# One mixer block on one core: two weight quarters loaded into the dead place of k, another split of the inverse shuffles, the normed input written later, and a new table of due times

## The chip, the cores and the metric

The kernel runs on one core of a Trainium2 chip. The metric is device time in microseconds (us): the median of three runs, 181.79 us, with 181.39 us the lowest and 182.12 us the highest. A profile was taken of one further execution. The engines are named as in the profile: PE (matrix multiplications; its weight loads are shown apart, as PEld), DVE (vector engine), ACT (scalar engine), POOL (GpSimd) and SP (which only issues DMAs here).

## The reference, cut to what matters

With S = 2048 positions and D = 448 channels, a gated long convolution is followed by a layer norm and an MLP that mixes positions:

```python
def _A_ref(q, k, v, shift_k, ssm_k, ssm_D):
    ...
        k_shift = k_shift + k_pad[:, t:t + S, :] * shift_k[:, ks - 1 - t][None, None, :]
    kv = k_shift * v
    ...
    y_f = kv_f * kf_f[None, :, :, :]
    ...
    y = y + kv * ssm_D[None, None, :]
    return q * y

def _B_ref(x, w1, b1, w2, b2):
    h = _layernorm(x, axis=-1)
    u = jnp.einsum("bsd,sf->bdf", h, w1) + b1
    u = _gelu(u)
    y = jnp.einsum("bdf,fs->bds", u, w2) + b2
    return (lambda x, *d: x.transpose(*d))(y, 0, 2, 1)

x = A_q
h = x + _A_ref(_layernorm(x, axis=-1), A_k, A_v, A_shift_k, A_ssm_k, A_ssm_D)
h2 = h + _B_ref(_layernorm(h, axis=-1), B_w1, B_b1, B_w2, B_b2)
```

W1 is 2048 x 1792 and W2 is 1792 x 2048, both bf16. The products y_f are a convolution of length 4096 along the positions; the kernel does it with small Fourier matrices on PE.

## The kernel before

**Layout.** Position s = 16 q + r lies in partition q (128 of them) and row r (R = 16 rows), so x, k and v are each 16 rows of 448 channels in every partition. All of SBUF is one tile, `arena`, cut by hand into byte ranges that are used again: k lies at bytes 0 to 14335 of each partition (`o_KH`), the transposed filter KT at 17024 to 31359, and the first half of W1 (`W1A`, hidden units 0 to 895, 16 rows of 1792 bytes) at 0 to 28671. So rows 0 to 7 of `W1A` cover exactly k, and rows 8 to 15 cover part of KT.

**Stages, in order.** (1) Inputs are loaded; k is transposed on PE (L936) and shifted, kv is formed (L955, L961). (2) "k1" and "u1": the first Fourier stage of the filter and of kv (L1015), copied out of PSUM (L1025), and moved between partitions by DMAs inside SBUF, the forward shuffles (L1031). (3) "k2" and "u2": the second stage (L1050). (4) "i1": sixteen products on DVE (L1083), eight groups of inverse matmuls (L1095) and sixteen copies out of PSUM (L717 when ACT does it, L720 when DVE does), each group giving two columns j = 2jj and 2jj+1 of `TU`. (5) Each column goes through an inverse shuffle into `TZ`: a big DMA from POOL for partitions 0 to 111 and a small one from SP for partitions 112 to 127 (L1119). The last pair of columns, 14 and 15, is split further by halves h (L1108): for h = 0 POOL issues both big DMAs and SP both small ones; for h = 1 POOL issues the big one of column 14, SP the big one of column 15, and ACT both small ones. The big DMAs fill rows 0 to 13 of `TZ` (group "zpool"), the small ones rows 14 and 15 ("zsp"). (6) "i2": the second inverse stage, two matmuls a row (L1215), reads a row of `TZ`. It can't begin before all big DMAs have landed, since each of them writes 8 partitions of all its rows. (7) Then for each row: times 1/sigma plus one (the gate, L1224 on ACT or L1226 on DVE), times (x - mean) (L1234), a sum and a sum of squares (L1262 on ACT), a chain of five small POOL operations for each pair of rows (L1272, L1275, L1277, L1282, and the power L1286), and the normed row Q (L1293). Rows 0 to 3 take another way: their normed x, `XN`, is prepared before (L1185 on ACT, L1187 on DVE; tag "xn") in the place of `TK`, and one operation (L1244) combines it with the matmul's result. Rows 0 and 1 have groups of their own with mean and variance from DVE (L1250, L1253, L1282), so POOL only has the power to do. (8) "mlp": seven accumulators in PSUM take Q row by row against `W1A` (L1340), then the other seven against `W1B` (L1350), GELU on ACT (L1330), and the second layer against W2 (L1362) with the last additions on DVE (L1365) and the stores.

**Statistics of x** (tag "q"): L1155 and L1157 on DVE, L1160 and L1163 on POOL, rows in pairs.

**Filler.** "warm" issues 34 matmuls whose result nobody uses (L1129), and "i2" two more groups of one; all of them are tied to one another in order.

**What sets the order.** Nothing is issued by hand. `op(...)` records each operation with what it reads and writes, and a planner (`schedule`) makes a list for each engine: whenever an engine is free in the planner's own clock, it takes, among the operations that are ready there, the one with the earliest due time; only among equal ones does the longer chain of work that hangs on it count. The due times are the table `WHEN`, one entry for each step of a tag. For operations that ACT or DVE can do, `WHERE` says a (ACT), d (DVE) or f (either, by the planner's clock). `after=` adds a full dependency, `safter=` one that only orders the planner's list. The lists are fixed in the program: on the chip an engine runs its list in order and waits with everything behind it when the next one isn't ready.

**W1 and W2.** `emit_w1_load` loads each half of W1 in four quarters of four rows (L1313 for `W1A`, L1317 for `W1B`), `emit_w2_load` W2 in four parts (L1324). All twelve are issued by SP and have `after=[shuf["zpool"]]`: none starts before the big inverse shuffles have landed.

Of the kernel before, what the change touches and what calls it, by code (L numbers as in the profile page):

```python
# [12 lines left out]
    "dummy": (69,),  # L13
    "tables": (172, 222, 238, 115, 211, 90, 258, 324,),
    "loads": (189, 214, 205, 290, 237, 82, 264, 277, 251, 276, 104, 283, 244, 317, 322,),
    "kv": (253, 110, 128, 123, 135, 121, 85, 66, 113, 159, 149, 191, 230, 266, 235, 142, 275,),
    "kT": (114, 112, 155, 152, 96, 80, 177, 176,),
    "k1": (188, 194, 229, 249, 190, 192, 213, 216, 218, 221, 227, 241, 185, 255, 269, 284,),
    "k2": (93, 139, 239, 168, 180, 225, 273, 295, 321, 320, 313, 314, 262, 293, 318, 315,),
    "u1": (250, 270, 274, 304, 287, 299, 311, 316, 268, 271, 296, 298, 301, 303, 306, 307,),  # L20
    "xload": (291, 182, 300, 223,),
    "ct": (100,),
    "bias": (178,),
    "q": (248, 233, 76, 233, 234, 329, 330, 332, 333,),
    "u2": (89, 97, 118, 141, 132, 137, 117, 91, 199, 164, 246, 219, 145, 156, 278, 281,),
    "i1": (151, 43, 55, 45, 52, 46, 58, 51, 74, 67, 64, 61, 150, 88, 56, 54,),
    "xn": (215, 265, 285, 232, 207, 256,),
    "w1a": (208, 148, 107, 323,),
    "w1b": (130,),
    "warm": (184, 183, 158, 65, 62, 83, 57, 125, 126, 127, 63, 59, 86, 209, 210, 187, 179, 106, 129, 167, 161, 157,  # L30
        153, 206, 193, 181, 196, 120, 101, 72, 32, 0, 47, 169,),
    "i2": (170, 1, 327, 10, 15, 6, 138, 4, 49, 9, 14, 3, 7, 243, 11, 2, 13, 17, 242, 25, 108, 103, 111, 282, 40, 163,
        220, 197, 12, 31, 257, 247, 286, 35, 60, 99, 312, 160, 140, 254, 308, 44, 41, 68, 22, 20, 98, 133, 245, 261,
        38, 29, 204, 289, 162, 18, 26, 240, 305, 294, 202, 154, 102, 263, 259, 201, 309, 39, 302, 328, 16, 147, 71,
        200, 326, 325, 27, 42, 30, 174, 94, 297, 75, 267, 195, 203, 331, 36, 272, 186, 260, 136, 92, 165, 24, 116,
        292, 217, 53, 231, 95, 70, 124, 105, 23, 48,),
    "w2": (198,),
    "mlp": (280, 166, 171, 212, 50, 28, 134, 122, 119, 226, 37, 112, 81, 21, 19, 5, 87, 144, 34, 84, 33, 131, 79, 8,
        146, 78, 77, 175, 224, 310, 109, 236, 228, 279, 143, 173, 252, 73, 288, 319,),
# [11 lines left out]
    "xn": "afdf",  # L51
    "i2": "fffadaaaaffd",
# [518 lines left out]
def _build(nc, A_q, A_k, A_v, A_shift_k, A_ssm_k, A_ssm_D, B_w1, B_b1, B_w2, B_b2, out):  # L571
# [5 lines left out]
    Bsz, S, D = A_q.shape  # L577
# [22 lines left out]
    o_TK = 31360  # L600
# [25 lines left out]
    with ctx:  # L626
        sch = _Sched(nc, ctx, n_dma_sems=112, small_off=SMALL)
        op = sch.op
# [97 lines left out]
        def emit_tables():  # L726
# [49 lines left out]
            for a, b_, c_ in ((0, 112, 14), (112, 128, 2)):  # L776
                op("pool", lambda e, W, a=a, b_=b_, c_=c_: e.iota(gcm[:, a:b_], [[0, 8], [512, c_]], base=512 * 14 * (a > 0),
# [5 lines left out]
            for k, (b0, st_) in enumerate(((2048, -2048), (2048, 2048), (0, 2048))):  # L783
                for a, b_ in (((0, 128),) if k == 0 else ((0, 112), (112, 128))):
                    op("pool", lambda e, W, k=k, b0=b0, st_=st_, a=a, b_=b_: e.iota(
                        cph[:, 128 * k + a:128 * k + b_], [[st_, 2], [0, (b_ - a) // 2]], base=b0, channel_multiplier=0),
                       w=[(o_gc + 1536 + 512 * k, 512, "cp%d" % k)], n=128, est=190.0)
# [252 lines left out]
        shuf = {}  # L1040
# [30 lines left out]
        i1_last = []  # L1071

        def emit_products_i1():
            for jj in range(R // 2):
# [16 lines left out]
                for h in range(2):  # L1091
# [7 lines left out]
                    evac(lambda jj=jj, h=h: TU[:, 2 * jj:2 * jj + 2, h, :], lambda b=bs[h]: Ppair(b),  # L1099
                         [(o_TU + (4 * jj + h) * DB, DB), (o_TU + (4 * jj + 2 + h) * DB, DB)], bs[h], 2 * D)  # L1100
                if jj == R // 2 - 1:
                    for h in range(2):
# [322 lines left out]
```

## Time and profile before

| what | value |
|---|---|
| median of the runs | 181.79 us |
| the profiled execution, its own time | 182.27 us |
| its span, first to last instruction | 180.2 us |
| share of the span busy: PE, DVE, ACT, POOL | 95%, 58%, 51%, 35% |
| matmuls of the MLP (L1340, L1350, L1362), number | 112, 112, 238 |
| SP issues all loads by | 9.4 us |
| first forward shuffle issued | 26.40 us |
| first inverse shuffle issued | 62.29 us |
| last big inverse shuffle issued by SP | 79.00 us |
| first matmul of i2 | 83.97 us |
| first weight DMA (L1313) issued | 83.94 us |

The span is what the instructions cover; the rest of the time of an execution, 2.07 us here, lies around it. PE's busy share is modelled, and shorter pauses of a matmul stream are hidden in it, so stages are best read from what an engine waited for. A wait is named after whatever came last by the profile.

### The profile page before, as it was taken

What the parts mean: (1) busy time and instruction counts of PE and PEld (TensorE: products, weight loads), DVE (VectorE), ACT (ScalarE), POOL (GpSimd) and SP (SyncE); (2) the same over time, 40 slices, a digit from 0 to 9 for tenths busy, and PEclk for the clock granted to TensorE, in tenths of its full rate; (3) what the DMA queues carried; (4) which work ended last, traced back from release to release, by engine and by line L of the source; (5) the groups of instructions that cost most, each with busy time, mean ns of one, the idle gap of its engine ahead of it and who ended that gap; (6) DMA issues with size and microseconds to landing.
All of it is one profiled execution on the core that took longest, in us unless ns stands there. A gap on an engine that the chain in (4) does not pass through costs nothing.

```text
span 180.2 us, 3395 instructions
## 1 busy us (share of the span) xinstructions
PE 170.7 (95%) x1333; PEld 97.5 (54%) x1333; DVE 104.8 (58%) x182; ACT 91.2 (51%) x129; POOL 63.2 (35%) x157
## 2 busy tenths in 40 slices
PE   6999999999889999898898999999999999999994
PEld 2888746543223332244343545556565677777784
DVE  7998677669889999999998645000000053322331
ACT  3897375689899999953985264710221100000000
POOL 8641209562950148797389953000000000000000
DMA  5997008686784947663999999990000001111122
GB/s 178 389 409 251 5 4 308 225 312 186 262 266 131 365 126 210 201 206 89 375 378 401 405 417 421 417 415 28 4 0 0 0 0 40 66 51 51 51 76 76
DMA packets 15347, 35.11 MB, mean 195 GB/s; under 512 B 3724, under 2 KB 9388, under 8 KB 15332
## 3 DMA queue, kind: packets, MB, share of 16 engines
q1 hardware_dynamic: 12068, 28.00, 41.8%
q0 software_dynamic: 3072, 6.80, 11.9%
q8 instruction: 10, 0.16, 0.4%
q10 hardware_dynamic: 192, 0.11, 0.2%
q14 instruction: 5, 0.04, 0.1%
HBM read 22.05 MB, written 1.84 MB: 133 GB/s over the span
## 4 chain that ended last, share of the span: by engine, by line
PE 65%; DVE 12%; ACT 10%; DMA 5%; POOL 3%; issue 2%; SPq 1%; DVEq 0%; POOLq 0%
PE ps L1362 23%; PE ps L1350 12%; PE ps L1340 9%; PE ps L955 7%; DVE arena L1083 5%; DMA arena<-arena 5%; PE ps L1015 4%; ACT arena L1025 4%; ACT arena L717 2%; PE ps L994 2%; PE ps L1050 2%; ACT arena L718 2%; PE ps L1095 1%; POOL arena L1286 1%; ACT arena L826 1%
## 5 line engine op out<-in xcount | busy, mean ns | idle before, releaser
L1362 PE MATMUL ps<-arena 128*128 128x448 bf16 (+2 forms) x238 | 43.5, 342 | 0.0
L1365 DVE SCALAR_TENSOR_TENSOR arena<-ps,arena 128x448 bf16<-128x448 f32 (+2 forms) x17 | 11.1, 656 | 54.2 <-PE ps L1362 54.2
L1362 PEld LDWEIGHTS ps<-arena 128*128 128x128 bf16 x238 | 32.9, 145 | 10.1 <-ACT arena L1330 0.8
L1340 PE MATMUL ps<-arena 128*128 128x448 bf16 x112 | 23.4, 353 | 0.6 <-DVE arena L1293 0.6
L1031 POOL DMA_DIRECT2D arena<-arena x32 | 17.5, 553 | 17.3 <-ACT arena L1025 16.3
L717 ACT CAST arena<-ps 128x896 bf16<-128x896 f32 x28 | 23.3, 979 | 0.4
L1350 PE MATMUL ps<-arena 128*128 128x448 bf16 x112 | 22.8, 352 | 0.0
L1025 ACT CAST arena<-ps 128x896 bf16<-128x896 f32 x22 | 18.9, 913 | 6.6 <-PE ps L1015 5.7
L1330 ACT ACTIVATE arena<-ps,arena 128x448 bf16<-128x448 f32 x14 | 8.3, 638 | 22.4 <-PE ps L1350 18.7
L1050 PE MATMUL ps<-arena 128*64 128x448 bf16 x128 | 16.0, 361 | 1.1 <-ACT arena L1025 0.7
L1340 PEld LDWEIGHTS ps<-arena 128*128 128x128 bf16 x112 | 10.6, 98 | 11.5 <-DVE arena L1293 2.2
L1083 DVE TENSOR_TENSOR arena<-arena 128x1792 bf16<-128x1792 bf16 x16 | 16.6, 1083 | 0.1
L1350 PEld LDWEIGHTS ps<-arena 128*128 128x128 bf16 x112 | 10.9, 98 | 10.1 <-DVE arena L1226 0.3
L1095 PE MATMUL ps<-arena 64*128 64x448 bf16 x128 | 14.1, 351 | 1.7 <-ACT arena L717 1.0
L1015 PE MATMUL ps<-arena 128*32 128x448 bf16 x256 | 14.8, 355 | 0.5 <-ACT arena L718 0.3
L955 PE MATMUL ps<-arena 112*128 112x224 bf16 (+3 forms) x112 | 13.4, 273 | 0.0
L1119 POOL DMA_DIRECT2D arena<-arena x14 | 8.3, 595 | 12.7 <-ACT arena L717 12.3
L955 PEld LDWEIGHTS ps<-arena 112*128 112x128 bf16 x112 | 9.2, 98 | 4.4 <-DVE arena L1025 0.9
L1050 PEld LDWEIGHTS ps<-arena 128*64 128x64 f16 x128 | 5.3, 108 | 11.4 <-ACT arena L717 3.7
L1262 ACT ACTIVATE arena<-arena 128x448 bf16<-128x448 f32 x14 | 8.1, 576 | 6.1 <-DVE arena L1234 6.0
L961 DVE TENSOR_TENSOR arena<-ps,arena 128x896 bf16<-128x896 f32 x8 | 8.6, 1089 | 4.3 <-PE ps L955 4.2
L1095 PEld LDWEIGHTS ps<-arena 64*128 64x128 f16 x128 | 5.0, 94 | 10.7 <-ACT arena L717 6.0
(93 smaller groups left out, 209.6 us busy)
## 6 DMA issues: line engine op xcount, KB each, us to landing
arena<-in_B_w_dram SPq DMA_DIRECT2D x8, 896.0 KB, 12.1
arena<-in_B_w_dram SPq DMA_DIRECT2D x2, 2048.0 KB, 17.0
arena<-arena SPq DMA_DIRECT2D x16, 224.0 KB, 3.2
arena<-arena POOLq DMA_DIRECT2D x32, 112.0 KB, 3.4
arena<-in_B_w_dram SPq DMA_DIRECT2D x2, 1536.0 KB, 19.5
arena<-arena POOLq DMA_DIRECT2D x14, 196.0 KB, 4.2
arena<-in_A_k_dram SPq DMA_DIRECT2D x4, 448.0 KB, 6.0
arena<-in_A_v_dram SPq DMA_DIRECT2D x4, 448.0 KB, 9.9
```

The costliest lines, as they stand in the source:

```text
L717: return e.copy(out=dst(), in_=src())
L955: op("pe", lambda e, W, b=b, i=i, cc=cc, dl=dl, i0=i0, i1=i1, rs=rs, sh=sh: e.matmul(Pb(b, i)[:, 112 * i0:112 * i1 + 112], KX[cc][0:112, i ...
L1015: op("pe", lambda e, W, b=b, r=r, q=q, x=x, c0=c0: e.matmul(PS[32 * q:32 * q + 32, b.slots[x], 0:D], E[:, 2 * r + x, c0:c0 + 32], src[:, r ...
L1025: return e.copy(out=dst, in_=Ppair(b)) if W == "act" else e.tensor_copy(out=dst, in_=Ppair(b))
L1031: shuf[tag].append(op(q_, lambda e, W, g=g, i=i, a=a, nu=nu, jh=jh: e.dma_start(T[a + i:a + i + 4 * nu - 3:4].rearrange("p (j k) c d -> p ...
L1050: op("pe", lambda e, W, b=bs[h], h=h, j=j, c=c, par=par: e.matmul(PS[64 * par:64 * par + 64, b.slots[c], 0:D], FW[:, 64 * c:64 * c + 64], ...
L1083: op("dve", lambda e, W, m=m, i=i: e.tensor_tensor(out=MR(m.slots[0]).rearrange("p (x y) d -> p x y d", x=2), in0=TU[:, i].unsqueeze(2).br ...
L1095: k = op("pe", lambda e, W, b=bs[h], m=ms[h], par=par, t=t, tab=tab, xy=xy, P=P: e.matmul(Pb(b, par), tab[P, :], MR(m.slots[0])[P, xy, :], ...
L1340: op("pe", lambda e, W, r=r, fc=fc, b=bs[fc]: e.matmul(Pb(b), W1A[:, r, 128 * fc:128 * fc + 128], Q[:, r, :], start=(r == 0), stop=(r == R ...
L1350: op("pe", lambda e, W, r=r, fc=fc, b=b: e.matmul(Pb(b), W1B[:, r, 128 * (fc - n0):128 * (fc - n0) + 128], Q[:, r, :], start=(r == 0), sto ...
L1362: op("pe", lambda e, W, r=r, fc=fc, b=b, d0=d0, d1=d1: e.matmul(Pb(b)[:, d0:d1], W2[fc // 7][:, fc % 7, r:S:R], G[:, fc, d0:d1], start=(fc ...
L1365: op("dve", lambda e, W, r=r, b=b, A=A, d0=d0, d1=d1: e.scalar_tensor_tensor(out=X[:, r, d0:d1], in0=Pb(b)[:, d0:d1], scalar=bm[:, r:r + 1 ...
```

## The change

Four edits and a new table.

**Early quarters.** The first two quarters of `W1A` (rows 0 to 7) lose the dependency on the inverse shuffles. What is left is that their place must have been read: the transposes of k's rows 0 to 7 for the first, of rows 8 to 15 for the second. SP still issues them in that order. The third and fourth quarter keep their dependency.

```diff
             for h in range(4):
                 sch.t0 = (T_W1 - 30.0 * (h > 1), T_WB - 30.0)[which] + 0.1 * h * (1 - which)
+                if which == 0 and h < 2:
+                    sch.t0 = -5.0 + h
...
-                       after=[shuf["zpool"]], safter=(wl[0],) if h else ())
+                       after=[shuf["zpool"]] if h > 1 else (), safter=(wl[0],) if h else ())
```

**Split of the inverse shuffles.** The big DMA of a column takes partitions 0 to 95 (rows 0 to 11 of `TZ`), the small one partitions 96 to 127 (rows 12 to 15). The tables that make the inverse matrices are written in the same two pieces.

```diff
-            for a, b_, c_ in ((0, 112, 14), (112, 128, 2)):
+            for a, b_, c_ in ((0, 96, 12), (96, 128, 4)):
...
-                            for q_, a, b_, j0 in (("sp" if h and par else "pool", 0, 112, 0), ("act" if h else "sp", 112, 128, 14)):
+                            for q_, a, b_, j0 in (("sp" if h and par else "pool", 0, 96, 0), ("act" if h else "sp", 96, 128, 12)):
...
-                    for q_, a, b_, j0 in (("pool", 0, 112, 0), ("sp", 112, 128, 14)):
+                    for q_, a, b_, j0 in (("pool", 0, 96, 0), ("sp", 96, 128, 12)):
```

**x normed later.** The four operations that write `XN` come after the last copy out of PSUM of i1 in the planner's list. Of the four, the first goes to ACT, the second and third to DVE, the fourth to either (before: ACT, either, DVE, either).

```diff
+        evl = []
...
-                    evac(lambda jj=jj, h=h: TU[:, 2 * jj:2 * jj + 2, h, :], lambda b=bs[h]: Ppair(b),
+                    ke = evac(lambda jj=jj, h=h: TU[:, 2 * jj:2 * jj + 2, h, :], lambda b=bs[h]: Ppair(b),
...
+                    evl.append(ke)
...
-                       w=[(o_TK + r * 4 * D, 4 * D)], n=D, est={"act": 590.0, "dve": 430.0})
+                       w=[(o_TK + r * 4 * D, 4 * D)], n=D, est={"act": 590.0, "dve": 430.0}, safter=evl)
...
-    "xn": "afdf",
-    "i2": "fffadaaaaffd",
+    "xn": "addf",
+    "i2": "aaffafaaddff",
```

**Due times.** Every entry of `WHEN` is another number, since the scale is another; what counts is their order. Among the steps from "tables" to "i1", with the loads of the weights, the order of any two is as before. It differs within and towards the tags "q", "xn", "warm", "i2" and "mlp". Of the long lines, these are the ones that are short or that are spoken of below:

```diff
-    "q": (248, 233, 76, 233, 234, 329, 330, 332, 333,),
+    "q": (2686.67, 2692.38, 2558.85, 2728.33, 2726.2, 2724.82, 2729.2, 2733.43, 2725.05,),
...
-    "xn": (215, 265, 285, 232, 207, 256,),
-    "w1a": (208, 148, 107, 323,),
+    "xn": (2725.33, 2727.89, 2403.48, 2719.09, 2605.55, 2614.65,),
+    "w1a": (2654.22, 2601.22, 2565.22, 2779.22,),
```

In "i2", some steps stand as follows (smaller is earlier; the two scales can't be compared with each other):

| step | before | after |
|---|---|---|
| matmuls of rows 0, 1, 2, 3 | 1, 49, 2, 242 | 0, 1089.89, 1529.56, 2230.1 |
| matmuls of rows 4, 5, 6, 7 | 197, 247, 44, 20 | 2583.72, 2265.39, 2533.39, 1092.93 |
| power of row 1's group (L1286) | 243 | 2662.27 |
| first POOL operations of the group of rows 2 and 3 (L1272, L1275, L1277) | 103 | 2744.56 |
| first POOL operations of the group of rows 4 and 5 | 99 | 2707.56 |
| power of the group of rows 4 and 5 | 160 | 2537.72 |

## The prediction

> **What bounds the kernel now.** I read the page first for the shape of the run, then the chain of waits, then tables by stage, then the waits inside the stages that the change touches.
>
> The page: PE carries most of the chain, and the DMA engines stand idle in slices 5 and 6 and are full from slice 20 on, when the weights come.
>
> ```profile
> span 180.2 us, 3395 instructions
> ...
> DMA  5997008686784947663999999990000001111122
> ...
> PE 65%; DVE 12%; ACT 10%; DMA 5%; POOL 3%; issue 2%; SPq 1%; DVEq 0%; POOLq 0%
> ```
>
> The table by stage (columns: window, its length, busy time of PE, PEld, DVE, ACT, POOL with counts, clock, DMA share, GB/s). The reader is to see three things: from 96.71 us PE is busy in all of 80.63 us, there is a hole in the DMA traffic around 20 to 24 us, and the traffic thins out in the last two microseconds before i2.
>
> ```profile
> 16.00:20.00 4.00, 4.00 (x40) 3.10 (x38) 2.40 (x7) 2.07 (x3) 1.80 (x4) 1.00 0.23 44
> 20.00:24.00 4.00, 4.00 (x53) 2.59 (x52) 2.81 (x5) 1.36 (x2) 0.00 (x0) 1.00 0.02 4
> ...
> 82.00:83.00 1.00, 1.00 (x7) 0.52 (x6) 1.00 (x4) 0.17 (x1) 0.74 (x3) 1.00 0.49 146
> 83.00:84.00 1.00, 0.44 (x4) 0.03 (x2) 1.00 (x5) 0.00 (x0) 0.83 (x2) 1.00 0.08 25
> ...
> 96.71:177.34 80.63, 80.63 (x437) 52.09 (x438) 20.37 (x43) 15.70 (x30) 10.17 (x26) 1.00 0.38 151
> ```
>
> The chain of waits from the end of i1 to i2 (start, length, what): a norm of x stands between the last two copies on ACT, but then the chain goes through SP, whose issues follow one another.
>
> ```profile
> 76.22 0.04 ACT arena L717
> 76.26 0.76 issue
> 77.02 0.77 ACT arena L1185
> 77.79 0.45 SPq L1108
> 78.24 0.04 issue
> 78.28 0.67 SPq L1108
> 78.95 0.04 issue
> 79.00 4.93 DMA arena<-arena
> ```
>
> PE's timeline from i2 on has only these two waits worth the name (last column: idle before, and its releaser):
>
> ```profile
> 89.36 0.55 PE L1215 MATMUL ps<-arena 128*128 128x448 bf16 x2 [0.68 <-ACT arena L1224]
> ...
> 96.71 0.55 PE L1340 MATMUL ps<-arena 128*128 128x448 bf16 x2 [0.58 <-DVE arena L1293]
> ```
>
> Behind the second stands POOL, which runs without a pause from 88.90 us. Its timeline: operations of the group of rows 2 and 3 (89.47) go ahead of the power of row 1 (89.97), and at 94.40 another group's first operation goes ahead of the power that rows 4 and 5 wait for.
>
> ```profile
> 89.47 0.54 POOL L1275 TENSOR_TENSOR arena<-arena 128x2 f32<-128x2 f32 x1
> 89.97 1.01 POOL L1286 TENSOR_TENSOR arena<-arena 128x1 f32<-128x1 f32 x1
> ...
> 94.40 0.54 POOL L1272 TENSOR_SCALAR arena<-arena 128x2 f32<-128x2 f32 x1
> 94.91 1.16 POOL L1286 TENSOR_TENSOR arena<-arena 128x2 f32<-128x2 f32 x1
> ```
>
> So what is left to win before the end is small and lies ahead of 96.71 us: an earlier start of i2, and PE's idle time between 83.97 and 96.71. In those 12.74 us PE starts 58 matmuls (26 of i2, 28 of L1340, 4 fillers); at 0.19 us each (32 of L1350 take 6.05 us in the chain) they are 11.0 us of work, so 1.7 us are idle. Neither number can be made much better than that.
>
> [...] the DMA share in 79 to 82 us is 0.66 to 0.76 and in 82 to 83 us 0.49 while shuffles are still under way. [...] between 79 and 82 us POOL's queue moved 0.54 MB and SP's 0.06 MB, and SP's got 0.10 MB through after 82 us, when POOL's had run dry. [...]
>
> **The change part by part.** All against the profiled execution (182.27 us; span 180.2 and 2.07 us around it). The median of the runs is 0.48 us lower; I take the same difference off both.
>
> *Early quarters of W1.* Removed after 83.94 us: two DMAs of 917,504 bytes, SP issues of 0.4 to 0.5 us each, and 1.84 MB of traffic, which at the 417 GB/s of the page's late slices is 4.4 us. Added before: the same two issues, each waiting for k's transposes (L936, the last starts at 15.3 us). Behind them on SP is the first forward shuffle at 26.40 us; SP's own waits show 17.0 us idle before it, so nothing is held up. Issue at about 15.6 us, some 2 us to the first bytes (a load of L1313 landed 4.7 us after issue in all, 2.2 of them transfer), 4.4 us transfer: landed at about 22 to 23 us, inside the hole. v's loads are ahead in SP's rings. Cost 0, hidden by that hole; if it closed, 4.4 us of traffic would lie on the forward shuffles, and I put 1 to 4 us on that. Gain: PE's waits after 83.97 us name the weights nowhere, L1313's first quarter landed at 88.6 us and the first L1340 ran at 89.75 after Q of row 0 (88.82 plus 0.48). The other weights land 4.4 us earlier, and nobody waits for them. So 0 by itself, bounds -0.2 and +0.3; what it gives is freedom to the lists.
>
> *Split 96 and 32.* Of each column POOL moves 168 KB instead of 196, SP 56 instead of 28; in the last pair SP's big one is 84 instead of 98, in front of it 28 + 28 instead of 14 + 14. Instructions stay the same in number: SP issues 16 rows in 0.671 and 112 rows in 0.684 us, POOL 0.587, so 0 there. The table pieces (L777, L780, L785) are as many, in idle time of POOL: 0. What moves is load between rings. i2's first rows need the big ones alone. POOL's queue has a seventh less, so it frees the engines earlier (0.14 x the 0.6 MB that it moved from 79 us on, at about 0.2 MB/us, is 0.4 us); SP's ring has from 76.14 us on 252 instead of 182 KB, 70 KB more, at the 0.10 MB that it moved in the 1.4 us after 82 us this is 1.0 us if all of it stands in front of the last landing. Bounds +1.0 and -0.4; I take 0 to +0.2, and 0.1 in the sum.
>
> *x normed later.* L1185 (0.76 us) leaves the place between the last two copies. The last copy starts at 77.68; its matmuls end at 77.09, so it may start 0.4 to 0.5 us earlier and end at about 78.15 instead of 78.57. SP's issues at 76.1, 76.9, 77.57, 78.28 and 79.00 are back to back, so with SP's order as it is this brings nothing. But among operations with the same due time the planner takes the one with the longer chain behind it, and the big DMA of column 15 has that; with its data ready before 78.28 it can go ahead of the second small one. Then it is issued 0.72 us earlier. Both ends: 0 and -0.72. As the landing is ruled by the rings too, I take -0.5. The norms go where ACT is idle (2.19 us before 80.76) and two on DVE at 0.56 each, which pushes two of the statistics (0.6 each) behind 84 us, where before two stood at 97.78 already; cost 0, 0.3 if they get in the way of the first combinations. Fillers: 32 ran from 77.19 to 83.42, so i2 can't start before that unless the list now holds fewer ahead of it.
>
> *New due times.* The matmuls of row 1 come second instead of after rows 2, 7 and 6; L1340 takes the rows in order, so row 1 is needed second. The power of row 1 now stands ahead of the first operations of rows 2 and 3, before behind them. That takes 0.49 + 0.54 us of L1272 and L1275 off its way (of this 0.6 us count, since row 1's variance came at 89.37 at the latest). The power of rows 4 and 5 stands ahead of the other groups' first operations: 0.54 us at 94.40. Some 1.1 us of POOL's order are thus won for exactly the rows behind which PE stood for 0.7 us at 96.71. Bounds: all 1.7 us of PE's idle time gained; or a new wait for one chain of a pair, 0.23 + 0.21 + 0.52 + 0.34 + 1.03 = 2.3 us, lost, since PE's order is fixed and holds everything behind the waiting matmul. I take -0.8.
>
> After 96.71 us PE is full whatever the order of L1340, L1350 and L1362, so that reordering is 0; the last row is still the one in two pieces, so the end after the last matmul stays.
>
> Sum: 0 + 0.1 - 0.5 - 0.8 = -1.2 us. 182.27 - 1.2 = 181.07; on the scale of the median 181.79 - 1.2 = 180.6 us.
>
> **The rivals.** 0.5% of 181.79 is 0.91 us, about what a measurement of this kernel can tell from no change.
> - *Hidden anyway*: SP's list keeps its order, i2 starts at 83.9, and POOL's order only moves the idle time. For it: PE is the bound for 80.63 of 93.37 us and waits for no weight. Against it: 1.7 us of idle time with named causes. 181.8 us, between 180.9 and 182.7.
> - *The ring of SP* (other side): its small shuffles double[...]. [...] i2 starts 1.0 us later, at 85.0 us: 182.8 us. For it: SP's queue is the last to finish. Against: the share of all DMA engines over 62 to 70 us is only 0.52 to 0.53. [...]
> - *A new wait in the fixed lists*: one exposed POOL chain, +2.3, less 0.4 from the start: 183.7 us. For it: PE's list is long and fixed. Against: the rows that PE needs first are now first.
> - *It doesn't do what it says*: the early loads slip behind 26.40 us and meet the forward shuffles, up to some 2 us more, 183.8 us. Against: SP has nothing else between 9.4 and 26.4 us.
>
> **How the numbers follow.** Forecast 0.46 (own range 179.2 to 180.9), hidden 0.30, ring 0.13, new wait 0.09, slipped 0.02. So faster by over 0.5% 0.46, within 0.5% 0.30, slower 0.24. The range 179.2 to 183.0 holds the first two, the ring's and the lower part of the others; below it lies only a case in which all 1.7 us and 0.9 us at the start are won.
>
> **What would show it.** L1313 twice at about 15.6 us, and landed before the first L1031; SP's third-last or second-last L1108 with 84 KB at about 78.3 us; first L1215 near 83.5 us; no wait of over 0.3 us for L1293 on PE; PE then without a pause for some 80 us. Wrong it would be if L1215 starts after 84.3 us, or if PE waits for DVE or POOL after 100 us.

## The result and the profile after

| | before | after |
|---|---|---|
| median | 181.79 us | 181.74 us |
| lowest and highest of the runs | 181.39 to 182.25 us (20) | 181.15 to 184.0 us (20) |
| ratio of the times, 95% interval | | 1.0 (0.9987 to 1.0013) |
| span of the profiled execution | 180.2 us | 180.5 us |

The number of runs stands in brackets; the one of 184.0 us had a lower granted clock (0.991) than all the others and is left out of the ratio.

So the time moved by nothing that can be told from no change, where 1.2 us less were forecast. The parts of the change are still all to be seen in the profile. Lines have moved: L914 is now L928 (the cast of b2), L1313 is L1331 (loads of `W1A`), L1031 is L1045 (forward shuffles), L955 and L961 are L969 and L975 (kv on PE and DVE), L1108 is L1124 and L1119 is L1135 (inverse shuffles), L1095 is L1110 (i1), L1129 is L1145 (fillers), L1215 is L1231 (i2), L1224 and L1226 are L1240 and L1242 (gates), L1262 is L1278 (sum of squares), L1272/75/77/82/86 are L1288/91/93/98/1302 (POOL's chain), L1293 is L1309 (Q), L1340, L1350 and L1362 are L1358, L1368 and L1380.

The page of after:

```profile
span 180.5 us, 3391 instructions
...
DMA  5999906696694937664999999900000010102022
...
PE 76%; ACT 13%; DVE 3%; DMA 2%; issue 2%; POOL 2%; DVEq 0%; POOLq 0%
```

Slice 5, which was idle, is full, and the full slices of the weights later are seven, before eight. The share of the DMA engines in the chain fell from 5 to 2%. The table by stage of after, with the columns of before:

```profile
16.00:20.00 4.00, 4.00 (x40) 3.05 (x38) 2.54 (x6) 2.12 (x3) 1.81 (x4) 1.00 0.93 259
20.00:24.00 4.00, 3.67 (x50) 2.59 (x51) 2.58 (x5) 0.95 (x3) 0.00 (x0) 1.00 0.66 244
...
94.07:177.60 83.53, 83.50 (x450) 52.99 (x451) 24.04 (x53) 16.79 (x35) 12.29 (x31) 1.00 0.35 138
```

The hole between 20 and 24 us is filled (244 GB/s, before 4), and from 94.07 us PE pauses for 0.03 us in all. But PE, which was busy in all of 20 to 24 us before, is so in 3.67 us of 4. The chain of waits into i2:

```profile
77.05 0.97 PE ps L1110 x8
78.02 0.05 issue
78.07 6.23 PE ps L1145 x32
84.29 0.05 issue
84.34 2.44 PE ps L1231 x12
```

SP is gone from it. The last matmul of i1 starts at 77.63 us here (76.75 before), i2 comes 6.71 us after it (7.22 before), and the fillers are now the last thing that the chain names ahead of i2. The first matmul of i2 starts at 84.34 us, beyond the 84.3 us that the prediction gave as a sign of being wrong. So i1 ended 0.9 us later, which is more than what was won behind it. PE's timeline of i2 has again two waits (idle before, releaser):

```profile
89.63 0.55 PE L1231 MATMUL ps<-arena 128*128 128x448 bf16 x2 [0.59 <-DVE arena L1242]
...
94.07 9.34 PE L1358 MATMUL ps<-arena 128*128 128x448 bf16 x48 [0.44 <-DVE arena L1309]
```

and from i2's first matmul to the last matmul it is 93.47 us against 93.54: the idle time has other places, but nearly the same sum. POOL's timeline ahead of the second wait is this:

```profile
90.64 0.60 POOL L1293 TENSOR_TENSOR arena<-arena 128x2 f32<-128x2 f32 x1 [0.60 <-ACT arena L1278]
91.33 0.34 POOL L1298 TENSOR_SCALAR arena<-arena 128x2 f32<-128x2 f32 x1
91.76 0.54 POOL L1288 TENSOR_SCALAR arena<-arena 128x2 f32<-128x2 f32 x1
92.26 1.16 POOL L1302 TENSOR_TENSOR arena<-arena 128x2 f32<-128x2 f32 x1
```

In before the same chain of rows 2 and 3 went on like this, after the power of row 1 (89.97, 1.01 us long):

```profile
90.95 0.20 POOL L1277 TENSOR_TENSOR arena<-arena 128x2 f32<-128x2 f32 x1
91.23 0.35 POOL L1282 TENSOR_SCALAR arena<-arena 128x2 f32<-128x2 f32 x1
91.66 1.03 POOL L1286 TENSOR_TENSOR arena<-arena 128x2 f32<-128x2 f32 x1
```

Row 1's Q comes 6.78 us after the start of i2 (7.05 before), but the first Q of rows 2 and 3, for which PE now waits, 9.11 us after it (8.76 before), and the other 9.60 us (9.80 before). The power of row 1 is out of this chain, but in its place POOL waits 0.60 us for ACT's sum of squares, and an operation of a later pair (91.76, 0.54 us) now stands ahead of the pair's power.

**Where the early part got longer.** DVE's timeline in the first stage of after:

```profile
17.58 1.09 DVE L975 TENSOR_TENSOR arena<-ps,arena 128x896 bf16<-128x896 f32 x1
20.45 0.18 DVE L928 CAST arena<-arena 128x16 f32<-128x16 bf16 x1 [1.78 <-DMA arena<-in_B_b_dram]
20.54 2.08 DVE L975 TENSOR_TENSOR arena<-ps,arena 128x896 bf16<-128x896 f32 x2
```

The cast of b2, an operation of 0.18 us whose result only the last layer needs, stands in DVE's list between the products that make kv. It waits for the last input in SP's ring (the queue of the DMAs that SP has issued; it was issued at 9.05 us in before), 4 KB in 128 packets, and the products wait behind it. In before the same wait was 1.46 us, and it ended 0.80 us after the last packet of that load (packets until 18.99 us, cast at 19.79). Here it ended 1.34 us after (19.11 and 20.45): the packets of `W1A`, in the same ring behind it, had been moving since 16.99 us. That became the theory: the early quarters delay the completion of b2. The first forward shuffle is issued 6.61 to 6.62 us after the cast both times (26.40 and 27.07 us). Where the cast comes early enough not to matter, this shuffle starts 10.84 us after the last of k's transposes has started; it was 11.08 us in before and 11.40 us in after. The theory accounts for these 0.32 us only. Of the rest of the 0.9 us by which i1 ended later, 0.35 us lie ahead of that transpose (15.67 us, 15.32 before; in all profiled executions below, with the quarters early or late, it starts between 15.32 and 15.68 us), and 0.21 us in the landing of one later forward shuffle (4.33 us in the chain of after, 4.12 in that of before).

### The profile page after: what moved, and what is told of

It reads as the page before. It is cut to its first block, busy times and chain, and to the rows that moved or that the text cites. A ratio compares the mean times of both kernels' runs of the same rounds, so it can differ in the third digit from the quotient of the medians.

```text
span 180.5 us, 3391 instructions
## 1 busy us (share of the span) xinstructions
PE 171.5 (95%) x1333; PEld 98.2 (54%) x1333; DVE 105.8 (59%) x184; ACT 89.6 (50%) x127; POOL 61.0 (34%) x157
## 4 chain that ended last, share of the span: by engine, by line
PE 76%; ACT 13%; DVE 3%; DMA 2%; issue 2%; POOL 2%; DVEq 0%; POOLq 0%
PE ps L1380 23%; PE ps L1368 12%; PE ps L1358 10%; PE ps L969 7%; ACT arena L731 6%; PE ps L1029 4%; ACT arena L1039 4%; PE ps L1145 3%; PE ps L995 3%; PE ps L950 3%; DMA arena<-arena 2%; PE ps L1008 2%; PE ps L1110 2%; PE ps L1064 2%; PE ps L1231 2%
## 5 line engine op out<-in xcount | busy, mean ns | idle before, releaser
L1380 PE MATMUL ps<-arena 128*128 128x448 bf16 (+2 forms) x238 | 43.7, 342 | 0.0
L1380 PEld LDWEIGHTS ps<-arena 128*128 128x128 bf16 x238 | 32.8, 145 | 10.4 <-ACT arena L1348 1.4
L1358 PE MATMUL ps<-arena 128*128 128x448 bf16 x112 | 23.3, 353 | 0.4 <-DVE arena L1309 0.4
L1045 POOL DMA_DIRECT2D arena<-arena x32 | 17.6, 555 | 17.7 <-ACT arena L1039 17.0
L1368 PE MATMUL ps<-arena 128*128 128x448 bf16 x112 | 22.3, 352 | 0.0
L1358 PEld LDWEIGHTS ps<-arena 128*128 128x128 bf16 x112 | 10.4, 98 | 11.4 <-DVE arena L1309 2.8
L1368 PEld LDWEIGHTS ps<-arena 128*128 128x128 bf16 x112 | 10.9, 98 | 10.0 <-ACT arena L1348 0.2
L1110 PE MATMUL ps<-arena 64*128 64x448 bf16 x128 | 13.9, 352 | 1.8 <-ACT arena L731 1.2
L969 PE MATMUL ps<-arena 112*128 112x224 bf16 (+3 forms) x112 | 13.4, 273 | 0.0
L1135 POOL DMA_DIRECT2D arena<-arena x14 | 8.1, 583 | 15.3 <-ACT arena L731 13.6
L1278 ACT ACTIVATE arena<-arena 128x448 bf16<-128x448 f32 x14 | 8.1, 577 | 8.0 <-DVE arena L1250 7.7
L969 PEld LDWEIGHTS ps<-arena 112*128 112x128 bf16 x112 | 9.2, 98 | 4.4 <-DVE arena L1039 0.8
L975 DVE TENSOR_TENSOR arena<-ps,arena 128x896 bf16<-128x896 f32 x8 | 8.6, 1090 | 4.3 <-PE ps L969 4.2
L1110 PEld LDWEIGHTS ps<-arena 64*128 64x128 f16 x128 | 5.0, 94 | 10.7 <-ACT arena L731 6.3
```

The costliest lines, as they stand in the source:

```text
L969: op("pe", lambda e, W, b=b, i=i, cc=cc, dl=dl, i0=i0, i1=i1, rs=rs, sh=sh: e.matmul(Pb(b, i)[:, 112 * i0:112 * i1 + 112], KX[cc][0:112, i ...
L1045: shuf[tag].append(op(q_, lambda e, W, g=g, i=i, a=a, nu=nu, jh=jh: e.dma_start(T[a + i:a + i + 4 * nu - 3:4].rearrange("p (j k) c d -> p ...
L1110: k = op("pe", lambda e, W, b=bs[h], m=ms[h], par=par, t=t, tab=tab, xy=xy, P=P: e.matmul(Pb(b, par), tab[P, :], MR(m.slots[0])[P, xy, :], ...
L1358: op("pe", lambda e, W, r=r, fc=fc, b=bs[fc]: e.matmul(Pb(b), W1A[:, r, 128 * fc:128 * fc + 128], Q[:, r, :], start=(r == 0), stop=(r == R ...
L1368: op("pe", lambda e, W, r=r, fc=fc, b=b: e.matmul(Pb(b), W1B[:, r, 128 * (fc - n0):128 * (fc - n0) + 128], Q[:, r, :], start=(r == 0), sto ...
L1380: op("pe", lambda e, W, r=r, fc=fc, b=b, d0=d0, d1=d1: e.matmul(Pb(b)[:, d0:d1], W2[fc // 7][:, fc % 7, r:S:R], G[:, fc, d0:d1], start=(fc ...
```

## The experiments

All medians of one group stand beside runs of the kernel before on the same chip. "Gap" is the time from the last matmul of i1 to the first of i2, "stretch" from there to the last matmul of all; both are from the one profiled execution of each kernel. The ratios are those on record and differ a little from the quotients of the medians.

### Each part of the change by itself (before: 181.83 us)

*Everything but the early quarters.* All four quarters of `W1A` again behind the inverse shuffles; only SP's list differs from that of the changed kernel.

```diff
-                       after=[shuf["zpool"]] if h > 1 else (), safter=(wl[0],) if h else ())
+                       after=[shuf["zpool"]], safter=(wl[0],) if h else ())
```

> The changed kernel with its first two quarters of W1 waiting for the inverse shuffles again; all other lists are the same. Theory A (the early load delays the landing of b2, for which DVE waits at 20 us, by 0.3 to 0.5 us, and so gives back what the shuffles won): 0.3 to 0.5 us faster than before, about 181.4; first forward shuffle 0.3 us or more earlier than in the changed kernel at the same pace of the k transposes. Rival (the later start of the forward shuffles was chance): as the changed kernel, 181.7 to 181.8. Second rival (the early quarters are needed by i2): slower than the changed kernel, with PE waiting for a weight before 96 us.

*The early quarters alone*, the same edit the other way round, in the kernel before.

> The kernel before with only the first two quarters of W1 freed from the inverse shuffles; all other lists are the same. Theory A: 0.3 to 0.5 us slower than before, and DVE's wait for b2 ends 0.3 to 0.5 us later. Rival (chance): the same as before, wait for b2 unchanged. If the early quarters help i2 by themselves: faster by 0.3 or more.

*The split alone*, 96 and 32 in place of 112 and 16, in the kernel before.

> The kernel before with only the split 96 and 32. The prediction's step: i2 starts 0.1 us later (bounds -0.4 and +1.0), time +0.1. The rival of SP's ring: i2 starts 1.0 us later, time +1.0.

*The later norms alone*: `safter=evl` on the four norms, in the kernel before.

> The kernel before with only the norms of x after the last copy of i1; SP's order stays small, small, big. If SP's back-to-back issues rule (the prediction's view of the unchanged order): last big DMA still issued 2.9 us after SP's first of the last group of four, i2 starts as before, time 0 to +0.2. Rival (the last copy rules): last copy 0.4 us earlier and i2 starts 0.4 us earlier, time -0.4.

| kernel | median | ratio to before (95%) | gap | stretch |
|---|---|---|---|---|
| all but the early quarters | 181.1 us | 0.9949 (0.9932 to 0.9966) | 6.60 us | 93.45 us |
| early quarters alone | 182.24 us | 1.002 (0.9994 to 1.0046) | 7.16 us | 93.53 us |
| split alone | 181.91 us | 1.0001 (0.9987 to 1.0016) | 7.65 us | 93.49 us |
| later norms alone | 181.86 us | 1.0 (0.9978 to 1.0023) | 7.01 us | 93.50 us |

The part that was to cost nothing is the one that costs. Without it the change is faster than before. By itself it looks 0.4 us slower, though the interval still holds no change. The split lengthens the gap by 0.43 us in its profiled execution, while its median is 0.08 us above that of before. Its chain of waits, to be held beside that of before:

```profile
77.95 0.80 SPq L1108
78.75 0.04 issue
78.80 5.23 DMA arena<-arena
```

The big DMA of column 15 is still SP's last one, and it takes 5.23 us from issue to landing where before it was 4.93; the other 0.13 us are in SP's issues. The later norms alone leave SP's order as it was (small, small, big), and the gap is 0.21 us shorter, with the same median. The order small, big, small of the changed kernel should then come from the table, which is tried below.

### Is it b2? (before: 181.74 us)

*The changed kernel once more*, as a measure.

> The changed kernel as it is, for the comparison with the next three on one chip. Theory A: 0 to 0.2 us off the kernel before, DVE's copy of b2 at 4.4 us or more after the start of the last k transpose (4.0 in the two quickest traces so far).

*The cast of b2 behind i1*, in the changed kernel, in before, and in the changed kernel without the early quarters. If b2's landing is all that the early quarters cost, they should cost nothing once no kv product stands behind the cast.

```diff
-            op("dve", lambda e, W: e.tensor_copy(out=b2c, in_=b2n), r=[(o_b2n, 32)], w=[(o_b2c, 64)], n=16)
...
+            sch.t0 = T_M1 + 30.0; op("dve", lambda e, W: e.tensor_copy(out=b2c, in_=b2n), r=[(o_b2n, 32)], w=[(o_b2c, 64)], n=16, after=i1_last[-1:])
```

> The changed kernel with DVE's copy of b2 put behind i1, so that nothing at 20 us waits for that small load; early quarters kept. Theory A (the early load costs only by way of this wait): at least as quick as with late quarters, 181.1 us or less, forward shuffles at most 10.5 us after the start of the last k transpose (10.84 to 11.40 so far). Rival (the early load costs elsewhere, or the cost is chance): 181.4 to 181.8.

> The kernel before with the same move of b2's copy and nothing else. DVE waited 1.0 to 1.5 us for it and the next kv product stands behind it. If that wait is on the path: 0.3 to 1.0 us faster, forward shuffles at most 10.5 us after the start of the last k transpose. If PE or the landing of the inputs is the limit there: the same.

> The changed kernel with late quarters and late copy of b2. Theory A: the same as with early quarters and late copy, within 0.2 us. Rival (the early load costs elsewhere): 0.5 us or more faster than with early quarters.

| kernel | median | ratio to before (95%) | gap | stretch |
|---|---|---|---|---|
| changed kernel again | 181.76 us | 1.0004 (0.9988 to 1.002) | 6.74 us | 93.46 us |
| changed, cast late | 181.69 us | 0.9991 (0.9977 to 1.0004) | 6.51 us | 93.80 us |
| before, cast late | 181.78 us | 1.0001 (0.9985 to 1.0018) | 7.17 us | 93.50 us |
| changed, quarters and cast late | 181.53 us | 0.999 (0.9977 to 1.0002) | 6.92 us | 93.73 us |

With the cast out of the way the early quarters cost 0.16 us (181.69 against 181.53, intervals of the ratios overlapping), where 0.66 us lay between the changed kernel here and the one without them above (181.76 less 181.1, on two chips), and the first forward shuffle starts 10.83 or 10.84 us after the last transpose in all three kernels with the late cast. That is what the theory wants. But two of its numbers failed: 181.69 us lies in the rival's range and not at 181.1 or less, and the shuffle comes 10.84 and not 10.5 us after the transpose, so something other than the cast holds it there. As a repair the moved cast fails: it made the planner write other lists for i2, and the stretch grew by 0.3 us. And in before there was little to win.

### The early quarters on one chip, and behind b2 (before: 182.01 us)

*All but the early quarters, again*, and *the changed kernel, again*, now side by side. (The chip is that of the first group, and not another one, as the expectation has it.)

> The changed kernel with all four quarters of W1A behind the inverse shuffles, once more and on another chip, beside the changed kernel (a_again2). Theory (the early quarters delay the landing of b2 and so DVE's kv products): 0.3 to 0.9 us less than the changed kernel, so 180.9 to 181.4 us, cast of b2 0.8 us after the last packet of its load. Rival (the 181.1 us of the first time was that chip or those executions): within 0.2 us of the changed kernel, 181.6 to 181.9 us.

> The changed kernel as it is, as the measure for its neighbours on this chip. Every theory: 181.6 to 181.9 us, cast of b2 1.25 to 1.35 us after the last packet of its load, i2 6.5 to 6.8 us after the last matmul of i1.

*Early, but only after b2 has landed*: the loads still go into k's dead place and fill the hole, but they are issued when b2's load (`b2d`) has landed. Only SP's list differs from the changed kernel's; in it b2's load has also changed places with that of b1 just ahead of it.

```diff
-            op(Dq, lambda e, W: e.dma_start(b2n, B_b2.rearrange("(q r) -> q r", r=R)), w=[(o_b2n, 32)], dmab=S * 2)
+            b2d.append(op(Dq, lambda e, W: e.dma_start(b2n, B_b2.rearrange("(q r) -> q r", r=R)), w=[(o_b2n, 32)], dmab=S * 2))
...
-                       after=[shuf["zpool"]] if h > 1 else (), safter=(wl[0],) if h else ())
+                       after=[shuf["zpool"]] if h > 1 else b2d, safter=(wl[0],) if h else ())
```

> The first two quarters still go into k's dead place before the forward shuffles, but SP issues them only when b2 has landed. Theory (all that the early load costs is b2's late landing): like a_late_again, 180.9 to 181.4 us, cast of b2 0.8 us after its last packet. Rival 1 (the early traffic costs by itself, whatever it overtakes): like a_again2, 181.6 to 181.9 us. Rival 2 (the loads, now 4 us later, meet the forward shuffles): 182 to 183 us, with the last forward shuffle landing over 0.5 us later.

*POOL's chains pair by pair*, without the early quarters: the first operations of a pair come in POOL's list after the power of the pair before (`lp` holds the powers so far).

```diff
-                       r=[(oh, 8)], w=[(oh + 16, 8)], est=290.0)
+                       r=[(oh, 8)], w=[(oh + 16, 8)], est=290.0, safter=lp[-1:])
```

> a_late_again with POOL's chains of the layer norm in strict order, one pair of rows after the other, so that no first operation of a later pair stands ahead of a power. Theory (POOL's order is what PE waits for in the first 13 us of i2, as the prediction had it): from the first matmul of i2 to the last of the MLP 0.3 to 0.7 us less than the 93.45 us of the changed kernel. Rival (PE is bound otherwise, by the copies of the gates and by the work there is): 93.3 to 93.6 us. Second rival (a strict order leaves POOL idle for a late pair): over 93.8 us.

| kernel | median | ratio to before (95%) | gap | stretch |
|---|---|---|---|---|
| all but the early quarters, again | 180.95 us | 0.9928 (0.9899 to 0.9957) | 6.50 us | 93.46 us |
| changed kernel, again | 181.69 us | 0.9977 (0.9957 to 0.9997) | 6.54 us | 93.44 us |
| early, after b2 | 181.07 us | 0.9936 (0.9906 to 0.9966) | 7.17 us | 93.45 us |
| all but the early quarters, pair by pair | 181.75 us | 0.9967 (0.9949 to 0.9985) | 6.50 us | 93.75 us |

The early quarters cost 0.74 us (181.69 less 180.95), and when they are issued after b2's landing 0.62 us of it is gone. The intervals of the ratios touch or overlap by a little, but the runs are well apart: nine of ten with the quarters behind b2 and all nine without early quarters took 181.47 us or less, 15 of the 22 of the changed kernel more. The same bytes go to the same place, and just in time: their packets moved from 20.75 us on, all but two of the 1024 were through by 26.47 us and the last at 27.73 us, and the first forward shuffle was issued at 26.32 us. So this run hardly tries what the quarters would cost beside the forward shuffles. (Its gap of 7.17 us is from an execution of 181.80 us, above its median, in which SP's big DMA landed 5.62 us after issue.) So it is not the bytes as such that cost, but that they are under way while b2's load completes. Whether it matters that they are in the same ring, or would cost the same from another queue, no run tells. DVE's waits between 15 and 28 us name b2's load (what waited for what: us in total, times, longest). Of the changed kernel on this chip:

```profile
DVE arena L928 <- DMA arena<-in_B_b_dram: 2.5, 1, 2.5
```

of the one without the early quarters:

```profile
DVE arena L928 <- DMA arena<-in_B_b_dram: 1.3, 1, 1.3
```

and of the one with the early quarters after b2:

```profile
DVE arena L928 <- DMA arena<-in_B_b_dram: 1.3, 1, 1.3
```

What the longer wait does to PE is in its timeline in the changed kernel on this chip:

```profile
22.10 0.79 PE L969 MATMUL ps<-arena 112*128 112x448 bf16 x5 [0.43 <-DVE arena L975]
23.43 1.49 PE L1029 MATMUL ps<-arena 128*32 128x448 bf16 x24 [0.53 <-DVE arena L734]
```

and in the table by stage, first of the changed kernel, then of the one without the early quarters (PE busy is the second number after the window):

```profile
20.00:24.00 4.00, 3.03 (x38) 2.06 (x40) 2.58 (x5) 0.58 (x1) 0.00 (x0) 1.00 0.66 239
```

```profile
20.00:24.00 4.00, 4.00 (x56) 2.90 (x54) 2.80 (x5) 1.34 (x3) 0.00 (x0) 1.00 0.02 4
```

The profiled executions together, each one a single execution (packets from the trace's packet records; the last column is from the start of k's last transpose to the first forward shuffle, 10.84 us where the cast doesn't hold it up):

| kernel | last packet of b2 | cast | difference | shuffle after transpose |
|---|---|---|---|---|
| before | 18.99 us | 19.79 us | 0.80 us | 11.08 us |
| all but the early quarters | 18.54 us | 19.34 us | 0.80 us | 10.84 us |
| the same, again | 19.01 us | 19.81 us | 0.80 us | 10.90 us |
| early quarters alone | 18.40 us | 19.65 us | 1.25 us | 10.84 us |
| changed | 19.11 us | 20.45 us | 1.34 us | 11.40 us |
| changed, again | 18.70 us | 20.03 us | 1.33 us | 11.07 us |
| changed, again, third group | 19.52 us | 20.87 us | 1.35 us | 12.13 us |
| early, after b2 | 19.03 us | 19.70 us | 0.67 us | 10.96 us |

The delay of about half a microsecond is there in each of the four with the quarters in the ring, and in no other. (With the cast moved away, the landing of b2 itself shows it: 1.30 us after the last packet with the early quarters, 0.78 and 0.79 us in the two kernels without.) Its effect varies, since b2's packets end anywhere between 18.4 and 19.5 us and by the difference of 10.84 and 6.61 us only a cast later than about 4.2 us after the transpose is felt; whenever it was later, the shuffle followed it by 6.61 or 6.62 us, in every profiled execution. The effect is from 0 to 1.29 us in these four, 0.52 us on average, against 0.13 us in the nine executions of this document whose cast stands in its old place and that have nothing behind b2 in the ring. That is 0.4 us of the 0.74; the other 0.3 us are not traced, and single executions of such a spread can't say more.

The strict order of POOL did not help. The wait ahead of the 48 matmuls of L1358 is gone, but PE's timeline has others in its place:

```profile
88.74 0.55 PE L1231 MATMUL ps<-arena 128*128 128x448 bf16 x2 [0.59 <-DVE arena L1242]
101.44 1.12 PE L1358 MATMUL ps<-arena 128*128 128x448 bf16 x5 [0.37 <-DVE arena L1309]
102.72 0.55 PE L1231 MATMUL ps<-arena 128*128 128x448 bf16 x2 [0.16 <-DVE arena L1242]
```

The stretch is 0.3 us longer, near what the second rival had (over 93.8 us). With this edit the planner also wrote other lists for PE, DVE and ACT, so the run doesn't show what POOL's order does alone. The other part of the 0.8 us by which this kernel is slower than its neighbour isn't in the stretch; in the one profiled execution b2 landed late (cast 4.81 us after the transpose), which may or may not hold for the others.

### The table alone, and the split without its fillers (before: 181.89 us)

*The new table alone*, in the kernel before. The expectation says that `WHERE` stays as before; in the kernel that ran it was the changed kernel's. With this table the edit of the norms changes the list of no engine, so this is also the changed kernel without the early quarters and without the split.

```diff
-    "xn": (215, 265, 285, 232, 207, 256,),
+    "xn": (2725.33, 2727.89, 2403.48, 2719.09, 2605.55, 2614.65,),
...
-    "xn": "afdf",
-    "i2": "fffadaaaaffd",
+    "xn": "addf",
+    "i2": "aaffafaaddff",
```

> The kernel before with the new table of due times and WHERE as before: no early quarters, no split, no edit of the norms. Theory (the table, not the edit of the norms, puts SP's big shuffle of column 15 ahead of the second small one; of i2 and the MLP it brings next to nothing): that big one is the second of SP's last three, i2 0.4 to 0.7 us nearer to the last matmul of i1 than the 7.2 us of before, from i2's first matmul to the last of all 93.4 to 93.6 us, so 181.1 to 181.5 us. Rival (the table works by its order of POOL's chains, as predicted): i2 to the end 0.5 to 0.8 us shorter than 93.54 us. Second rival (table and edits only work together): 181.6 us and more.

*Two fillers fewer ahead of i2*, without the early quarters:

```diff
-        N_WZ, N_WI, N_W0, N_WK, N_WJ = 34, 1, 9, 3, 1
+        N_WZ, N_WI, N_W0, N_WK, N_WJ = 30, 1, 9, 3, 1
```

> a_late_again with 30 fillers in the first group instead of 34, so that 30 and not 32 stand ahead of i2; the fillers compute nothing that is used. Theory (the fillers end where the shuffles land, at about 4.9 us after SP's big one is issued): i2 6.2 to 6.6 us after the last matmul of i1, time within 0.3 us of a_late_again's 180.95 us. Rival (only the fillers hold i2): i2 6.1 us after it, 0.4 us faster.

*The same with the split of before*, 112 and 16.

> a_late_f30 with the inverse shuffles split 112 and 16 as in the kernel before. Theory (the split loads SP's ring, 0.4 us in b_split, and this is what rules the landing): i2 0.2 to 0.4 us nearer to the last matmul of i1 than in a_late_f30, 180.5 to 180.8 us. Rival 1 (with the big one ahead of the second small one the split no longer counts): the same as a_late_f30 within 0.1 us. Rival 2 (the split helps there, since POOL's queue has less): 0.2 to 0.4 us later.

| kernel | median | ratio to before (95%) | gap | stretch |
|---|---|---|---|---|
| new table alone | 184.38 us | 1.0135 (1.0113 to 1.0157) | 6.92 us | 96.22 us |
| 30 fillers, 96 and 32 | 181.69 us | 0.9991 (0.9976 to 1.0005) | 6.57 us | 93.81 us |
| 30 fillers, 112 and 16 | 180.82 us | 0.9944 (0.9923 to 0.9964) | 6.34 us | 93.45 us |

The first half of the first expectation holds: with the table alone SP issues the big DMA of column 15 as the second of its last three, and the gap is shorter, though by 0.30 us where 0.4 to 0.7 were expected. So the table, not the edit of the norms, moved it. The time does not hold: 2.5 us slower than before, all in the stretch. PE's timeline there (in this kernel L1229 is i2, L1238 and L1240 are gates, L1354 and L1307 the first half of the MLP and Q):

```profile
88.95 0.55 PE L1229 MATMUL ps<-arena 128*128 128x448 bf16 x2 [1.15 <-ACT arena L1238]
90.16 0.66 PE L1354 MATMUL ps<-arena 128*128 128x448 bf16 x2 [0.66 <-DVE arena L1307]
...
103.33 0.55 PE L1229 MATMUL ps<-arena 128*128 128x448 bf16 x2 [0.68 <-DVE arena L1240]
```

and its windows around the second wait (the last but two is the granted clock):

```profile
87.05:90.46 3.41, 1.60 (x8) 0.43 (x6) 3.40 (x14) 3.41 (x9) 2.65 (x5) 1.00 1.04 387
90.46:93.87 3.41, 3.41 (x11) 1.35 (x10) 2.80 (x9) 2.99 (x9) 3.16 (x7) 0.50 1.05 384
```

From 90.46 to 93.87 us PE's clock was 0.50; in the 3.41 us ahead of that it was 1.00, with PE busy for 1.60 us. That the waits lowered it isn't shown. The three waits are 2.49 us, where before had 1.26 us in two. It is tempting to add the halved clock, 1.7 us of work lost by an estimate from these 3.41 us, and so to make up the 2.68 us by which the stretch is longer. But of the five executions of this kernel only three show a lowered clock (0.991 over the span: 184.13, 184.22 and 184.38 us); the two with a full clock took 184.53 and 184.67 us and were no faster. So what the halving costs isn't shown, and how the waits make 2.68 us stays open. With this table the new split, or the old one with 30 fillers, has a stretch of 93.45 us. So table and edits only work together, the second rival of that expectation; why isn't shown.

With 30 fillers the gap is 6.57 us, no shorter than with 34 (6.60 and 6.50 us), and i2 starts 5.11 us after the issue of SP's big DMA, with 34 fillers 5.15 and 5.05 us. So fillers and landing end at the same place, and the rival by which only the fillers hold i2 (6.1 us) failed. The time failed too: 181.69 us is 0.74 us above 180.95, where 0.3 was the most, and the stretch is 0.35 us longer.

The last pair tells what the split costs now: the gap is 0.23 us shorter with 112 and 16. From the issue of SP's big DMA to i2 it is 4.89 us (78.01 to 82.90), with 96 and 32 it is 5.11 us (77.90 to 83.01). This is the theory's lower end, from one profiled execution each. The difference of the medians, 0.87 us, is more than that, since 0.36 us of it lies in the stretch, where the two have different lists (PE waits 0.77 us for L1309 in one and 0.18 us in the other), and some 0.3 us in neither.

Three versions are the fastest: without the early quarters (180.95 us), with them behind b2 (181.07 us), and without them, with the old split and 30 fillers (180.82 us). Their ratios to before, 0.9928, 0.9936 and 0.9944, have overlapping intervals, so which is best isn't settled. Each is 0.9 to 1.1 us below before.

## Why the prediction was wrong, step by step

- **Early quarters**: "Cost 0, hidden by that hole". This is the step that failed. The loads were issued at 15.92 and 16.36 us (0.3 us later than said), filled the hole and landed at 22.19 and 24.45 us (22 to 23 was said), before the first forward shuffle; and they cost 0.74 us, above the bound of +0.3. The prediction named who is ahead in SP's rings (v's loads) and who is behind (the forward shuffle), but asked nobody's wait for what lands inside the hole. b2's load was the last in the ring, DVE's list had its cast among the kv products, and the trace of before showed the wait of 1.46 us for it. The price put on a closed hole, 1 to 4 us on the forward shuffles, was not tried: with the loads after b2 all but two of their packets were through when the first of those had just been issued, and they cost 0.12 us, which is within the noise. How the later loads delay b2's completion, and where the 0.3 us of the cost lie that b2's cast doesn't explain, stays open.
- **Split 96 and 32**: +0.1 was taken, within +1.0 and -0.4. Alone it lengthened the gap by 0.43 us, and under the new order by 0.23 us, in one profiled execution each; its own median moved by 0.08 us. Right in kind (with more in SP's ring the big DMA landed 5.23 us after its issue, before 4.93), and by the gap too small in size; the rival called the ring of SP had 1.0 us, an estimate.
- **x normed later**: -0.5, for the big DMA going ahead of a small one. It did, and together with the split the gap is 0.51, 0.48 and 0.68 us shorter in three profiled executions of the changed kernel, where the two steps had -0.4. The cause was half wrong: the table did it, and the norms' edit alone left SP's order as it was. The floor that the prediction gave, the fillers, is what the chain names now, but with four fewer of them i2 came no sooner (a gap of 6.57 us against 6.60 and 6.50), since the shuffles land there too.
- **New due times**: "I take -0.8". The second step that failed; measured -0.07 to -0.10 us in the stretch. Row 1's Q gained 0.27 us of the 0.6 and the first of rows 2 and 3 lost 0.35. The step counted the POOL operations that left a chain and not what would come in their place: in the chain of rows 2 and 3 a wait of 0.60 us for ACT's sum of squares and 0.54 us of a later pair's operation. ACT and `WHERE`, changed too, were in no term of the sum. And the first of PE's two waits (0.68 us before, 0.59 after) is for a gate, which none of the POOL operations counted reaches. The rival of a new wait in the fixed lists had 2.3 us; it didn't come in the changed kernel, but the same table without the split gave 2.68 us in the stretch. What would shorten this idle time stays open: the strict order of POOL didn't, and it moved the other engines' lists too.
- **After the first waits** PE ran without a pause for 83 us, and no wait of PE for DVE or POOL came after 100 us. The wait for L1309 was 0.44 us, where under 0.3 was said.
- **POOL's queue at 82 us**: it had not run dry there. From 79 to 82 us 318 packets of POOL's queue passed, 0.54 MB, and 75 of SP's, 0.06 MB; from 82 to 84 us POOL's queue moved 46 more, 0.06 MB, beside 117 of SP's, 0.10 MB. In which order the packets of the two queues were taken isn't shown.

The sum: 0.74 for the quarters, -0.48 to -0.68 for the start and about -0.08 for the stretch make -0.02 to +0.18 us, and -0.05 was measured. So "hidden anyway" had the time by luck and not by its reason: without the early quarters the change brought 0.73 and 1.06 us, and the step that was taken as free gave all or most of it back.

## What to carry to other kernels

A hole in the DMA traffic was not free in this kernel, since something small that an engine waits for landed in it: filling it cost 0.74 us, and 0.12 us with the bulk loads issued after that landing. So look up which loads are still under way when the bulk load is issued, who waits for them, and what is queued behind that waiter, and issue the bulk load after their landing. Take operations on late inputs out of the list of an engine that has urgent work behind them (DVE stood 1.46 us at b2's cast in before, 1.78 us in after), but look at what that does to the rest of a planned list. In this kernel a table of due times was worth something only together with the code it was made for: the same table brought 0.1 us at most in the stretch with the new split and cost 2.68 us without it. When a step takes operations out of one engine's chain, ask what that chain waits for next.

## What the hardware showed

- A DMA of 4 KB completed 0.80 to 0.81 us after its last packet where SP issued nothing behind it until the forward shuffles (nine executions, by the cast that waits for it), 0.67 us after it where it had changed places with b1's load, and 1.25 to 1.35 us after it when two loads of 0.9 MB followed in the same ring (four executions). By which mechanism the later loads go with a later completion, and whether it takes the same ring, no run shows.
- In the profiled execution of the new table alone PE's clock was 0.50 from 90.46 to 93.87 us. In the stretch just as long ahead of it (87.05 to 90.46 us, clock 1.00) PE was busy for 1.60 us of 3.41, its longest single pause being 1.15 us. In the kernel before PE was busy for 2.73 us of that same window, and the clock was 1.00 there and in the 3.41 us after. What lowered the clock isn't shown. Nor is its cost: two of the five executions of the new table alone had a full clock and were no faster (184.53 and 184.67 us against 184.13 to 184.38).
